# Strassen's products over 1024 tokens instead of 512 for the last four token chunks, with half of g kept in DRAM meanwhile

## The chip, the cores and the metric

The kernel runs on one core of a Trainium2 chip. The metric is the device time of one execution in microseconds (us), lower is better; it is measured several times, and the median is compared. One further execution is recorded by the hardware profiler; its instructions, waits and transfers are what the views of the profile show. Engines are called as there: PE is the matrix engine (PEld its weight loads), DVE the vector engine, ACT the scalar engine, POOL the general one, SP the queue from which nearly all DMAs are issued.

## The reference

Windowed attention over 8 batches and 8 heads of 576 tokens, then a gated feed-forward layer over all 4608 tokens. The part that matters here is the second:

```
x   = attention(q, k, v) as [4608 tokens, 512]
h   = x @ w_in                      # [4608, 2048]
g   = h * erf(softplus(h))
out = g @ w_out                     # [4608, 512]
```

## The kernel before

**Precision.** Every matmul of the feed-forward layer is made of three: each operand is split into a rounded part (hi) and the rest (lo), and hi*hi, hi*lo and lo*hi are summed in PSUM. DVE and ACT make these parts: a copy that rounds gives hi, a subtraction on DVE gives lo.

**Chunks and steps.** The 4608 tokens are taken in nine chunks of 512 (TOK), numbered 0 to 8. A chunk has eight steps (SPC), one for each pair of 128-wide feature tiles of the 2048 features; STEPS lists all 72 in order. In step t PE multiplies the pair's h (mm1, or mm1_fast from chunk 3 on, FAST), DVE takes h out of PSUM (take, take_fast), ACT makes softplus (argument, L664) and erf (table, L667), each with a table load, DVE multiplies both into g (gate, L674) and splits g in ghi (L677) and glo (L678), and PE multiplies g by w_out into four PSUM banks, acc[0] to acc[3], one for each 128 tokens (mm2, L692). mm2 runs two steps behind mm1. A step is two visits of the main loop, x = 2t and 2t+1; each has a part of mm1, then 12 of the step's 24 matmuls of mm2, each 512 columns wide.

**Strassen's products.** From chunk 3 on, the pair of feature tiles is computed by Winograd's form of Strassen's scheme: w_in's pair is cut in two by features and by contraction, x in two by contraction and by tokens (halves of 256 tokens, HN). Seven products replace eight. A product is 6 matmuls (two halves of its contraction by three for hi and lo), 256 columns wide (L639), so 42 such matmuls a step, 24 in the first visit and 18 in the second. Their PSUM banks are h and bank ("tx" in the profile). The sums of w_in are built once, kept in DRAM (ws) and loaded for each step (load_left, 1024 KB and 768 KB). The sums of x are made for each chunk by DVE (right_less, right_lo) and ACT (right_hi) from x loaded by right_load in up to 12 DMAs.

**Attention** is spread over the feed-forward layer. It has 72 units. The table PACE lists the visits x at which two units have their turn ("a visit with attention"): PE turns two units' probabilities (L253), multiplies values (L272) and makes two later units' scores (L214); DVE takes maxima (L225), ACT the exponents (L235), DVE and POOL normalize (L246 to L248). In before the last visit with attention is x = 103, in step 51.

**Order.** All engines run their own instructions in the order in which the code issues them (manual_schedule); SP too starts its DMAs one after the other, and a DMA whose source or room is not ready holds up those behind it. When a chunk's sums are complete, store (L719) copies acc[0] and acc[2] out on DVE, acc[1] and acc[3] on ACT, and sends them to DRAM; between one chunk's last mm2 and the next chunk's first there is always a part of mm1.

Of the kernel before, what the change touches and what calls it, by code (L numbers as in the profile page):

```python
# [18 lines left out]
P = 128  # L19
# [24 lines left out]
SCALE = 0.125  # L44
BIG = 3.0e38

# [10 lines left out]

RUNS = [(0, 0, HALF), (1, 0, SPC), (0, HALF, SPC)] + [(c, 0, SPC) for c in range(2, NCH)]
STEPS = [(c, p, i) for i, (c, a, b) in enumerate(RUNS) for p in range(a, b)]
# [23 lines left out]

PACE = [19, 23, 27, 31, 33, 35, 37, 39, 43, 47, 51, 55, 59, 61, 65, 67, 71, 75, 79, 83, 87, 91, 93, 97, 99, 103]


def visits():


    at = {n - FIRST: [n] for n in range(FIRST, 2 * NBLK + LAG)}  # L90
    n, x = 2 * NBLK + LAG, 2 * HALF + 1
    for k in range(3):
        at[x + 5 * k // 2] = [n + k]
    for x, n in zip(PACE, range(n + 3, NU + LAG, 2)):
        at[x] = [i for i in (n, n + 1) if i < NU + LAG]
    assert max(n for ns in at.values() for n in ns) == NU + LAG - 1
    return at


def ends(t):  # L100

    return t + 1 == NT or STEPS[t][2] != STEPS[t + 1][2]
# [34 lines left out]
def attn_moe_kernel(ctx: ExitStack, tc: tile.TileContext, qk, v, masks, eye, w_in, w_out, out):  # L137
# [29 lines left out]
    pz = [one.tile([P, n], F32, name=f"pT{i}") for i, n in enumerate((2 * P, TOK))]  # L167
    plain = one.tile([P, 2 * TOK], F32, name="plain")

# [48 lines left out]
    def mask_max(u):  # L218

        pr = probs[u] = work.tile([P, 2 * PARTS, KEYS], F32, name="prob", bufs=LAG + 1)  # L220
        nmax = maxes[u] = small.tile([P, 2 * PARTS], F32, name="nmax", bufs=LAG + 1)
        for h in range(2):
            for p in range(PARTS):
                g = PARTS * h + p
                nc.vector.tensor_tensor_reduce(  # L225
                    out=pr[:, g, :], in0=sps[h][:, u % 2, p, :], in1=mask[QUADS.index(kinds(u, p))],
                    scale=-SCALE, scalar=BIG,
                    op0=ALU.add, op1=ALU.min, accum_out=nmax[:, g:g + 1],
                )
# [341 lines left out]
    def load_left(t, j):  # L571
        if t < NT and STEPS[t][0] >= FAST:
            at = slice(0, PART * KIND) if j == 0 else slice(PART * KIND, len(LEFT) * KIND)
            nc.sync.dma_start(out=left(t).bitcast(F32)[:, at], in_=ws[STEPS[t][1]][:, at])

# [50 lines left out]
    def right(x):  # L626

        c, at = divmod(x + READY, 2 * SPC)
        if FAST <= c < NCH:
            for job, *args in JOBS.get(at, ()):  # L630
                job(c, *args)
# [34 lines left out]
    def table(t):  # L666
        nc.scalar.activation(out=ls[t], in_=ls[t], func=AF.Erf)  # L667

    def gate(t, j):

        hc, e = hs[t], ls[t]
        if j == 0:
            gs[t] = []
            nc.vector.tensor_tensor(out=e, in0=hc, in1=e, op=ALU.mult)  # L674
        ghi, glo = (work.tile([P, TOK], F32R, name=n) for n in ("ghi", "glo"))
        gs[t].append((ghi, glo))
        nc.vector.tensor_copy(out=ghi, in_=e[:, j])  # L677
        nc.vector.tensor_tensor(out=glo, in0=e[:, j], in1=ghi.bitcast(F32), op=ALU.subtract)  # L678

    def mm2(t, j):  # L680
        ghi, glo = gs[t][j]
        _, ftp, run = STEPS[t]
        ft = ftp * PAIR + j
        first, last = ftp == RUNS[run][1] and j == 0, ends(t) and j == PAIR - 1
        parts = ((ghi, wout_hi), (ghi, wout_lo)), ((glo, wout_hi),)

        if last:
            parts = (sum(parts, ()),)
        for part in parts:
            for tt in range(TOK // P):  # L690
                for g, w in part:
                    nc.tensor.matmul(acc[tt], g[:, tt * P:(tt + 1) * P], w[:, ft, :],  # L692
                                     start=(first and w is wout_hi and g is ghi),
                                     stop=(last and g is glo))
        if j == PAIR - 1:
            del gs[t]

# [21 lines left out]
    def store(c):  # L719
        last = c == NCH - 1  # L720
        for tt in range(TOK // P):
# [3 lines left out]
            else:  # L725
                if tt == 0:
                    o = doubles(2).bitcast(F32).rearrange("p n w -> p (n w)")[:, 0:DM]
                else:
                    o = io.tile([P, DM], F32, name="w", bufs=4)
                copy_for(tt)(out=o, in_=acc[tt])  # L730
            r = c * TOK + tt * P
            (nc.scalar if last and tt % 2 else nc.sync).dma_start(out=out[r:r + P, :], in_=o)

    with tc.manual_schedule():
# [14 lines left out]

        plan = visits()  # L750

# [9 lines left out]
        todo, scaled, fresh = [], [FIRST - 1], []  # L761
        for x in range(2 * (NT + 2)):
            t, j = divmod(x, 2)
# [60 lines left out]
            load_left(t + 2, j)  # L824
            right(x)
            build(x)
            for n in ns:
# [5 lines left out]
            if x == 4 * SPC - 2:  # L833
                load_x(2, range(twice))
            for u in [u for u in scaled if due[u] == x + 1]:
                scaled.remove(u)
                normalize(u)
            for m in ready:
                finish(m)
        assert not todo and not prep and not staged and not begun and not made and not rest  # L840

# [83 lines left out]
```

## Time and profile before

| | us |
|---|---|
| median of 3 runs | 907.95 (907.29 to 909.37) |
| the profiled execution, its own time | 909.89 |
| the profiled execution, its span | 907.8 |

The span runs from the first to the last instruction; 2.1 us of the profiled execution's own time lie outside it. The own time is 1.94 us above the median of the runs. Rows of a view name line, engine, operation, what is written and read, and the count. In a timeline the first number is the start, the second how long it took; matmuls overlap, so that the distance of two starts, not the length of one, tells what a matmul costs PE's time. In rows of stretches, the numbers are busy times of PE, PEld, DVE, ACT and POOL, then the granted clock of PE, the busy share of the DMA engines and GB/s.

### The profile page before, as it was taken

The page shows a single profiled execution, that of the slowest core. Times are in us where ns is not written, and L with a number is a line of the kernel's source. Part 1 is how long each engine was busy: PE and PEld are TensorE (multiplying, and loading weights), DVE is VectorE, ACT ScalarE, POOL GpSimd, SP SyncE. Part 2 cuts the span into 40 slices and gives each one's busy share as a digit, 9 for nine tenths or more (in the row PEclk, how much of TensorE's full clock was granted, in tenths as well). Part 3 has the DMA queues.
Part 4 walks back from the last instruction along what each step waited for, and adds up shares of the span by engine and source line. Part 5 has one row for each costly group of instructions (what it writes and reads, how often), then busy time and mean ns, then how long its engine had stood idle before and what let it go on. Part 6 is the DMA issues. An engine that isn't in the chain of part 4 may idle for free.

```text
span 907.8 us, 22886 instructions
## 1 busy us (share of the span) xinstructions
PE 886.3 (98%) x9142; PEld 754.2 (83%) x9142; DVE 669.4 (74%) x1703; ACT 600.5 (66%) x1266; POOL 76.9 (8%) x97
## 2 busy tenths in 40 slices
PE   7799999999999999999999999999999999999998
PEld 3467777888887888889988988888988999999996
DVE  5888878876788888667876777678666866776555
ACT  6889879876678687666776676669654644545442
POOL 2312100000011100000100000001000000000000
PEclk9899999999999999999999999999999999999999
DMA  8874444432459688777658765877566546656521
GB/s 276 278 258 151 123 164 130 155 109 94 156 190 330 216 304 296 245 274 233 217 212 284 264 211 189 290 262 256 179 242 230 181 149 230 235 176 205 200 82 47
DMA packets 69450, 188.89 MB, mean 208 GB/s; under 512 B 9184, under 2 KB 17632, under 8 KB 63200
## 3 DMA queue, kind: packets, MB, share of 16 engines
q1 hardware_dynamic: 69056, 186.91, 60.5%
q8 instruction: 72, 1.18, 0.5%
q10 hardware_dynamic: 288, 0.52, 0.1%
q14 instruction: 34, 0.28, 0.1%
HBM read 153.85 MB, written 33.55 MB: 206 GB/s over the span
## 4 chain that ended last, share of the span: by engine, by line
PE 85%; DVE 7%; ACT 3%; DMA 3%; issue 1%; POOL 0%; SPq 0%; DVEq 0%; POOLq 0%; ACTq 0%
PE acc L692 40%; PE h L639 15%; PE tx L639 12%; PE h L518 10%; PE sp L272 3%; PE sp L214 3%; DMA dbl<-in_w_in_dram 2%; PE sp L253 1%; ACT prob L235 1%; PE h L354 1%; DVE s L674 1%; DVE hc L660 1%; PE acc L272 1%; DVE ghi L677 0%; DVE w L455 0%
## 5 line engine op out<-in xcount | busy, mean ns | idle before, releaser
L692 PE MATMUL acc<-wout_hi,ghi 128*128 128x512 f32 x576 | 228.4, 397 | 0.4 <-DVE ghi L677 0.2
L692 PE MATMUL acc<-wout_lo,ghi 128*128 128x512 f32 x576 | 225.6, 392 | 0.0
L664 ACT ACTIVATE s<-hc 128x1024 f32<-128x1024 f32 x72 | 76.5, 1062 | 188.5 <-DVE hc L653 171.1
L692 PE MATMUL acc<-wout_hi,glo 128*128 128x512 f32 x576 | 159.0, 389 | 0.0
L692 PEld LDWEIGHTS acc<-wout_hi,glo 128*128 128x128 f32 x576 | 108.1, 188 | 22.8
L692 PEld LDWEIGHTS acc<-wout_hi,ghi 128*128 128x128 f32 x576 | 108.5, 188 | 20.6 <-DVE ghi L677 0.8
L692 PEld LDWEIGHTS acc<-wout_lo,ghi 128*128 128x128 f32 x576 | 108.6, 189 | 19.6
L248 POOL TENSOR_TENSOR prob<-prob,rinv 128x256 f32<-128x256 f32 x72 | 69.2, 971 | 536.0 <-DVE ssum L246 313.7
L678 DVE TENSOR_TENSOR glo<-s,ghi 128x512 fp32r<-128x512 f32 x144 | 100.0, 694 | 5.5 <-PE acc L692 0.5
L235 ACT ACTIVATE prob<-prob,nmax 128x64 f32<-128x64 f32 x288 | 96.4, 339 | 8.3 <-DVE nmax L225 7.8
L674 DVE TENSOR_TENSOR s<-hc,s 128x1024 f32<-128x1024 f32 x72 | 92.9, 1290 | 9.1 <-ACT s L667 9.0
L639 PE MATMUL h<-win 128*128 128x256 f32 x720 | 98.1, 283 | 0.0
L518 PE MATMUL h<-x,win 128*128 128x512 f32 x384 | 96.6, 393 | 1.5 <-DVE hc L660 1.5
L664 ACT ACT_TABLE_LOAD x72 | 92.4, 1283 | 1.3
L667 ACT ACT_TABLE_LOAD x72 | 92.4, 1283 | 1.3
L639 PEld LDWEIGHTS h<-win 128*128 128x128 f32 x720 | 91.6, 192 | 0.0
L518 PEld LDWEIGHTS h<-x,win 128*128 128x128 f32 x384 | 71.2, 188 | 17.5 <-DVE hc L660 2.3
L667 ACT ACTIVATE s<-s 128x1024 f32<-128x1024 f32 x72 | 76.3, 1060 | 0.8
L677 DVE CAST ghi<-s 128x512 fp32r<-128x512 f32 x144 | 68.4, 475 | 3.1 <-PE acc L692 0.6
L225 DVE CUSTOM_DVE_ANT_0 prob<-sp,cst 128x64 f32<-128x64 f32 x288 | 45.3, 219 | 33.9 <-ACT rows L314 20.8
L314 ACT COPY rows<-sp 128x128 f32<-128x128 f32 (+7 forms) x167 | 27.9, 307 | 57.1 <-PE sp L214 54.9
L649 DVE TENSOR_TENSOR hc<-h,hc 128x512 f32<-128x512 f32 x48 | 33.2, 692 | 41.2 <-PE h L639 40.9
(108 smaller groups left out, 1259.4 us busy)
## 6 DMA issues: line engine op xcount, KB each, us to landing
win<-ws SPq DMA_DIRECT2D x48, 1024.0 KB, 5.8
win<-ws SPq DMA_DIRECT2D x48, 768.0 KB, 4.4
v<-in_v_dram SPq DMA_DIRECT2D x72, 256.0 KB, 4.3
qk<-in_qk_dram SPq DMA_DIRECT2D x48, 272.0 KB, 4.1
dbl<-in_w_in_dram SPq DMA_DIRECT2D x16, 512.0 KB, 4.8
dbl<-in_w_out_dram SPq DMA_DIRECT2D x16, 512.0 KB, 3.7
ws<-x SPq DMA_DIRECT2D x32, 256.0 KB, 4.2
qk<-in_qk_dram SPq DMA_DIRECT2D x24, 288.0 KB, 4.4
```

What stands on the lines that cost most here:

```text
L225: nc.vector.tensor_tensor_reduce(out=pr[:, g, :], in0=sps[h][:, u % 2, p, :], in1=mask[QUADS.index(kinds(u, p))], scale=-SCALE, scalar=BIG ...
L235: nc.scalar.activation(out=probs[u][:, j, :], in_=probs[u][:, j, :], func=AF.Exp, scale=-1.0, bias=nmax[:, j:j + 1], accum_out=sums[u][:, ...
L248: nc.gpsimd.tensor_tensor(probs[u], probs[u], rinv.broadcast_to([P, 2 * PARTS, KEYS]), op=ALU.mult)
L272: nc.tensor.matmul(xp[h * D:(h + 1) * D, qs], vt[ks, s, h, :], pt[ks, h * P + s * STRIP:h * P + (s + 1) * STRIP], start=True, stop=True, t ...
L518: nc.tensor.matmul(h, win_at[:, ftp, j, cc // 2, w, cc % 2, :], x[cc], start=(k == 0 and i == 0), stop=(k == CC - 1 and i == 2))
L639: nc.tensor.matmul((h, bank)[b][:, half * HN:(half + 1) * HN], w[:, k, wi, c, :], x[:, xi, c, :], start=(c == 0 and n == 0), stop=(c == 1 ...
L664: nc.scalar.activation(out=ls[t], in_=hs[t], func=AF.Softplus)
L667: nc.scalar.activation(out=ls[t], in_=ls[t], func=AF.Erf)
L674: nc.vector.tensor_tensor(out=e, in0=hc, in1=e, op=ALU.mult)
L677: nc.vector.tensor_copy(out=ghi, in_=e[:, j])
L678: nc.vector.tensor_tensor(out=glo, in0=e[:, j], in1=ghi.bitcast(F32), op=ALU.subtract)
L692: nc.tensor.matmul(acc[tt], g[:, tt * P:(tt + 1) * P], w[:, ft, :], start=(first and w is wout_hi and g is ghi), stop=(last and g is glo))
```

## The change

Chunks 0 to 4 stay as they are (PAIRED = 5). Chunks 5 to 8 become two pairs, 5 with 6 and 7 with 8. For a pair, the seven products are made over 1024 tokens, so that a token half is a whole chunk of 512: 7 products of 6 matmuls, 512 columns wide, give h of one pair of feature tiles for both chunks, called A (the first chunk) and B (the second). The eight feature pairs of a pair of chunks are eight such batches, d = 0 to 7 and 8 to 15.

There is room in PSUM for one chunk's sums only. So g of A is multiplied by w_out at once, and g of B is written to DRAM (kept_g, 512 KB for each feature pair) and read back later (load_g).

The main loop now ends at step 40's start, and a new loop of 34 periods follows. ITEMS lists what mm2 does in each: the last two steps of chunk 4 (periods 0 and 1), A of the first pair (2 to 9), B of it (10 to 17), A of the second (18 to 25), B of it (26 to 33). Products are made in periods 0 to 7 and 16 to 23 (BIG); periods 8 to 15 and 24 to 33 hold mm2 alone, 24 matmuls. In a period with products, groups of them (third) alternate with quarters of mm2 (6 matmuls). The sums of x for the second pair are made in periods 8 to 15 (AFT), those of the first pair in visits 68 to 79 and period 0 (FORE). load_g of an item is issued two periods ahead, at the period's end; the store of B's g is issued after multiply_big of B.

All attention that went with steps 40 to 51 is moved: PACE has visits at shorter distances up to x = 65, and what remains goes into periods 0 to 4.

The diff, cut to what matters:

```diff
-PACE = [19, 23, 27, 31, 33, 35, 37, 39, 43, 47, 51, 55, 59, 61, 65, 67, 71, 75, 79, 83, 87, 91, 93, 97, 99, 103]
+PACE = [17, 21, 23, 27, 29, 31, 33, 35, 37, 39, 43, 47, 49, 51, 53, 55, 57, 59, 61, 63, 65]
+BIG = {**{d: d for d in range(SPC)}, **{d + SPC: d for d in range(SPC, 2 * SPC)}}
+ORDER = ("A11", "A12", "S2", "S3", "A22", "S1", "S4")
...
+    def big_load(i):
...
+        for place, name in RAW.items():
+            place, k, c = name, int(name[1]) - 1, PAIRED + 2 * i + int(name[2]) - 1
+            for c2 in range(2):
+                a, end = c * TOK, (c + 1) * TOK
+                while a < end:
+                    b, s0 = divmod(a, S)
+                    m = min(end - a, S - s0)
+                    nc.sync.dma_start(out=raw[place][c2][:, a - c * TOK:a - c * TOK + m],
+                                      in_=xT[b][2 * k + c2][:, s0:s0 + m])
+                    a += m
...
+    AFT = {0: [LO["T4"], LO["T1"]], 8: [(big_load, 1)], 9: [LESS["T1"] + (room_v,)],
...
+    ITEMS = [NT - 2, NT - 1] + [(kind_, i * SPC + k) for i in range(2) for kind_ in "AB" for k in range(SPC)]
+
+    def mm1_big(d, k):
+        bank_ = (h, bank)[(7 * d + k) % 2]
...
+        for c in range(2):
+            for n, (wi, xi) in enumerate(((0, 0), (0, 1), (1, 0))):
+                nc.tensor.matmul(bank_, w[:, wi, c, :], x[c][:, xi, :],
+                                 start=(c == 0 and n == 0), stop=(c == 1 and n == 2))
...
+    def multiply_big(kind_, d):
+        e = hs[kind_, d]
+        nc.vector.tensor_tensor(out=e, in0=e, in1=ls[kind_, d], op=ALU.mult)
+        gs[kind_, d] = []
+        if kind_ == "B":
+            nc.sync.dma_start(out=kept_g[d // SPC][d % SPC], in_=e)
+
+    def load_g(item):
+        kind_, d = item
+        if kind_ == "B":
+            e = work.tile([P, PAIR, TOK], F32, name="hc") if d % 4 > 1 else slab(d % 4)
+            nc.sync.dma_start(out=e, in_=kept_g[d // SPC][d % SPC])
+            hs[item] = e
+
+    def split_item(item, j):
+        e = ls[item] if item == NT - 2 else hs[item]
+        split(item, e[:, j], nc.scalar.copy if isinstance(item, tuple) and item[0] == "B" else None)
...
+        if d is None:
+            groups = [()] * 4
+        elif BIG.get(i + 1) is None:
+            groups = [(0, 1, 2), (3, 4), (5, 6), ()]
+        else:
+            groups = [(0, 1), (2, 3), (4, 5), (6,)]
...
+        split_item(item, 1)
+        third(0)
+        jobs(AFT.get(i, ()))
+        quarter()
+
+        third(1)
+        for u in pending:
+            exponents(u)
...
+            for kind_ in "AB":
+                e = ls[kind_, behind_]
+                nc.scalar.activation(out=e, in_=e, func=AF.Erf)
+        quarter()
...
+            multiply_big("A", behind_)
...
+        turn(ready)
+        if ahead is not None:
+            split_item(ahead, 0)
+        last_ = 6 in groups[2]
+        if last_:
+            multiply_big("B", behind_)
+        third(2)
+        if i and behind_ is not None and not last_:
+            multiply_big("B", behind_)
+        quarter()
+
+        third(3)
+        quarter()
+        if done(item) is not None:
+            store(done(item))
+        attend(ready, scored)
+        if d is not None:
+            load_left(NT + d + 2, 1)
+        if i + 2 < len(ITEMS) and isinstance(ITEMS[i + 2], tuple):
+            load_g(ITEMS[i + 2])
...
-        for x in range(2 * (NT + 2)):
+        for x in range(2 * NT):
...
+            jobs(FORE.get(x, ()))
...
+        for i in range(len(ITEMS)):
+            period(i, late)
```

At the first join of A and B, this is how it stands on two engines. On PE, in before, from chunk 7's last sums to chunk 8's first (acc_93 to acc_96 are acc[0] to acc[3], tx and h are the banks of the products):

```order
L692 MATMUL acc_96<-wout_hi,ghi 128x512
L692 MATMUL acc_96<-wout_lo,ghi 128x512
L692 MATMUL acc_96<-wout_hi,glo 128x512
L639 MATMUL tx<-win 128x256 x12
L639 MATMUL h<-win 128x256 x12
L692 MATMUL acc_93<-wout_hi,ghi 128x512
```

On PE, in the changed kernel, from period 9 (A, d = 7) to period 10 (B, d = 0):

```order
L712 MATMUL acc_96<-wout_hi,ghi 128x512
L712 MATMUL acc_96<-wout_lo,ghi 128x512
L712 MATMUL acc_96<-wout_hi,glo 128x512
L712 MATMUL acc_93<-wout_hi,ghi 128x512
L712 MATMUL acc_93<-wout_lo,ghi 128x512
```

No product stands between the last sums of A and the first of B any more. On SP, in before, at the same join of chunks 7 and 8 (win<-ws is load_left):

```order
L574 DMA win<-ws 128x1536
L574 DMA win<-ws 128x2048
L732 DMA out_dram<-dbl_10030 128x512
L732 DMA out_dram<-w 128x512 x3
L574 DMA win<-ws 128x1536
```

On SP, in the changed kernel, from period 8 to period 10 (plain<-xT is the last DMA of big_load, g_112<-hc the store of B's g for d = 7, dbl_8496<-g_112 and dbl_8544<-g_112 are load_g of B for d = 0 and 1):

```order
L776 DMA plain<-xT_108 128x512
L872 DMA g_112<-hc 128x1024
L878 DMA dbl_8496<-g_112 128x1024
L750 DMA out_dram<-o 128x512
L750 DMA out_dram<-w 128x512 x3
L878 DMA dbl_8544<-g_112 128x1024
L878 DMA hc<-g_112 128x1024 x2
```

B's first load stands behind the 12 DMAs of big_load and the store of B's last g, and its second load behind the four stores of A's chunk. On DVE, in the changed kernel, in periods 8 and 9 (hc<-hc,s is multiply_big of B for d = 7, then the second split of A's last g, two sums of x in v_85 and v_86, the first split of B's first g, and store's copies):

```order
L869 TENSOR_TENSOR hc<-hc,s 128x1024
L687 CAST ghi<-hc 128x512
L688 TENSOR_TENSOR glo<-hc,ghi 128x512
L783 TENSOR_TENSOR v_85<-win 128x512
L783 TENSOR_TENSOR v_86<-win 128x512
L688 TENSOR_TENSOR glo<-dbl_8496,ghi 128x512
L748 COPY o<-acc_93 128x512
L748 COPY w<-acc_95 128x512
```

The copies of A's sums out of PSUM stand behind the split of B's first g.

More of the change, by code (lines that the diff above doesn't have):

```diff
@@ L691, in mm2, with mm @@
                 for g, w in part:
[L692 to L696, printed above, removed]
+                    yield dict(out=acc[tt], lhsT=g[:, tt * P:(tt + 1) * P], rhs=w[:, ft, :],
+                               start=(first and w is wout_hi and g is ghi), stop=(last and g is glo))
+    def mm2(t, j):
+        _, ftp, run = STEPS[t]
+        for args in products(t, ftp * PAIR + j, j, ftp == RUNS[run][1] and j == 0, ends(t) and j == PAIR - 1):
+            mm(args)
+    def mm(args):
+        nc.tensor.matmul(args["out"], args["lhsT"], args["rhs"], start=args["start"], stop=args["stop"])
     partial = dram.tile([TOK // P, P, DM], F32, name="partial")
```

194 lines of the change are left out of this document (167 added, 27 removed).

## The prediction

> **What bounds the kernel now.** First the page: its busy shares, then the chain that ended last, then single steps.
>
> ```profile
> PE 886.3 (98%) x9142; PEld 754.2 (83%) x9142; DVE 669.4 (74%) x1703; ACT 600.5 (66%) x1266; POOL 76.9 (8%) x97
> PE 85%; DVE 7%; ACT 3%; DMA 3%; issue 1%; POOL 0%; SPq 0%; DVEq 0%; POOLq 0%; ACTq 0%
> ```
>
> PE is busy 98% of the span, and 85% of the chain that ended last is PE's. DVE and ACT have a quarter and a third of the span free. That says what bounds, not how densely PE works. For that I took one step of chunk 7 without attention, as a stretch and on PE's timeline, and for comparison a visit of chunk 1, where products are 512 columns wide.
>
> ```profile
> 756.25:766.77 10.52, 10.52 (x68) 9.54 (x67) 6.20 (x11) 4.69 (x5) 0.00 (x0) 1.00 0.65 228
> 756.25 1.60 PE L639 MATMUL tx<-win 128*128 128x256 f32 x12
> 757.68 1.60 PE L639 MATMUL h<-win 128*128 128x256 f32 x12
> 759.12 0.40 PE L692 MATMUL acc<-wout_hi,ghi 128*128 128x512 f32 x1
> ...
> 146.77:152.21 5.44, 5.44 (x25) 4.50 (x24) 5.30 (x10) 5.39 (x14) 0.00 (x0) 1.00 0.65 209
> 148.13 1.52 PE L518 MATMUL h<-x,win 128*128 128x512 f32 x6
> 149.49 0.39 PE L692 MATMUL acc<-wout_hi,ghi 128*128 128x512 f32 x1
> ```
>
> The step takes 10.52 us, with no gap on PE, at a granted clock of 1.00, while DVE works 6.20 and ACT 4.69 of it. So a step's time is the sum of its matmuls, and only two things move the end: the time PE needs for its matmuls, and gaps in its row. From start to start, twelve 256-column matmuls take 759.12 − 757.68 = 1.44 us, 0.120 each. Six of 512 columns take 149.49 − 148.13 = 1.36 us, and the visit's 24 take 5.44: 0.2267 each. Twice 0.120 is 0.240: 13 ns more than one of 512.
>
> **Part 1, wider products: −10.2 us.** The last four chunks are 32 steps of 10.52 us, 336.6 us. Afterwards PE has 16 sets of 7 x 6 = 42 matmuls for products and 32 items of 24 for mm2, all 512 wide: (672 + 768) x 0.2267 = 326.4 us. Difference 10.2 us. From the 256-wide matmuls alone it is 672 x 0.0133 = 8.9; the rest goes with the changes between widths, which also end. So 8.9 to 10.2; I take 10.2, since whole stretches show it.
>
> The Trainium skill ("TensorE: Matmul & The Clock Gate", section on 56 against 53.3 ns) gives warm matmuls N columns at 2.4 GHz plus about 2.5 ns fixed each, by which the joining would save 672 x 2.5 ns, 1.7 us. The rows above show 13 ns, so the trace does not agree, and the measured spacing goes into the sum.
>
> **Part 2, the joins of A and B: +9.5 us.** In before, one part of mm1 covers the copying of a chunk's sums:
>
> ```profile
> 660.49 1.69 PE L639 MATMUL tx<-x,win 128*128 128x256 f32 x12
> 660.57 0.68 DVE L730 COPY dbl<-acc 128x512 f32<-128x512 f32 x1
> 661.17 0.68 DVE L730 COPY w<-acc 128x512 f32<-128x512 f32 x1
> 663.45 0.40 PE L692 MATMUL acc<-wout_hi,ghi 128*128 128x512 f32 x1
> ```
>
> PE comes back to acc 2.96 us after the chunk's end. At the start of periods 10 and 26 that cover is gone, and B's first g must come from DRAM. Its load stands on SP behind the store of B's last g, which waits for a long row of work on DVE and ACT. The prices:
>
> ```profile
> L678 DVE TENSOR_TENSOR glo<-s,ghi 128x512 fp32r<-128x512 f32 x144 | 100.0, 694 | 5.5 <-PE acc L692 0.5
> L674 DVE TENSOR_TENSOR s<-hc,s 128x1024 f32<-128x1024 f32 x72 | 92.9, 1290 | 9.1 <-ACT s L667 9.0
> L677 DVE CAST ghi<-s 128x512 fp32r<-128x512 f32 x144 | 68.4, 475 | 3.1 <-PE acc L692 0.6
> L649 DVE TENSOR_TENSOR hc<-h,hc 128x512 f32<-128x512 f32 x48 | 33.2, 692 | 41.2 <-PE h L639 40.9
> L664 ACT ACTIVATE s<-hc 128x1024 f32<-128x1024 f32 x72 | 76.5, 1062 | 188.5 <-DVE hc L653 171.1
> L667 ACT ACT_TABLE_LOAD x72 | 92.4, 1283 | 1.3
> L667 ACT ACTIVATE s<-s 128x1024 f32<-128x1024 f32 x72 | 76.3, 1060 | 0.8
> L609 ACT CAST win<-w 128x512 fp32r<-128x512 f32 x15 | 8.4, 615 | 0.0
> ...
> 902.07 0.69 DVE L730 COPY dbl<-acc 128x512 f32<-128x512 f32 x1 [2.71 <-PE acc L692]
> 902.79 0.34 SPq L732 DMA_DIRECT2D out_dram<-dbl  x1
> ```
>
> I count from the start of period 7 (23 for the second pair). A product or a quarter of mm2 is 6 x 0.2267 = 1.36 us. The period holds 66 matmuls, 14.96 us, and periods 8 and 9 have 24, 5.44 each: period 10 is due at 25.84. PE ends the fifth product at 6 x 1.36 = 8.16. Then DVE has, in its order: the fifth take 0.69, A's multiply 1.29, a split 0.475 + 0.694, B's multiply 1.29, the sixth take (1024 columns; no row has it, the nearest is the multiply's 1.29), the seventh 0.69: 14.6. ACT: softplus of B 1.06, table 1.28, erf of A 1.06: 18.0. DVE: multiply of A 1.29, split 1.17, multiply of B 1.29: 21.7. The last two rows show a handover: the copy ends at 902.76, SP issues at 902.79 and takes 0.34. With that issue, of the store, before the load's, the load starts at 22.1.
>
> ```profile
> dbl<-in_w_in_dram SPq DMA_DIRECT2D x16, 512.0 KB, 4.8
> dbl<-in_w_out_dram SPq DMA_DIRECT2D x16, 512.0 KB, 3.7
> DMA to landing us min/median/max: 3.4/4.8/6.7
> 686.04 7.64 SPq L597 DMA_DIRECT2D win<-xT  x12
> L732 SPq DMA_DIRECT2D out_dram<-w x26: 333/410/1702, 219.4 to 904.2; - x26
> ```
>
> Loads of 512 KB, the size of load_g, land after 3.4 to 6.7 us. With the 512 KB store just ahead I take the larger median, 4.8, for the second pair. In the first pair the 2 MB of big_load are ahead too, issued from about 13 on (they stand behind the store of B's g for d = 6, whose multiply ends at 8.16 + 0.69 + 1.29 + 1.17 + 1.29 = 12.6); I take the middle of 4.8 and 6.7. So the loads land at 26.9 and 27.9. After that ACT makes ghi (0.62), DVE glo (0.69), and only then, by DVE's order, the copy of acc[0] (0.68), with handovers 2.2 us. PE starts at 29.1 and 30.1 instead of 25.84: gaps of 3.3 and 4.2 us.
>
> The second load waits on SP for four stores, the last of which needs copies that end 2.8 us after the first landing; at 0.41 us an issue it starts 3.7 after that landing, lands 4.25 later (middle of the medians), and its ghi is there 0.7 later: at 8.65, when PE, started at 2.2, has ended period 10 at 7.64. Gap 1.0 at each pair. Later loads find four buffers and run ahead. Sum 3.3 + 4.2 + 2 x 1.0 = 9.5. Bounds: all loads at 3.4 give 2 x (1.9 + 0.2) = 4.2; all at 6.7 give 2 x (5.2 + 3.5) = 17.4.
>
> The Trainium skill ("DMA: Bandwidth & Descriptors", anatomy of one DMA) fits 2.0 us plus bytes at 436 GB/s on another queue than SP, an estimated 3.2 us for 512 KB, by which the joins would cost some 3.4 us. No load of that size here landed under 3.4.
>
> **Part 3, hurried attention: +1.2 us.** Each visit's PE work stays the same, but it has to fit in fewer steps: visits only two apart (one step) are seven instead of four before x = 48, and nine instead of two up to x = 65.
>
> ```profile
> 249.62:257.46 7.84, 7.84 (x158) 6.43 (x156) 5.88 (x14) 4.45 (x4) 2.02 (x2) 1.00 0.20 75
> 263.05:271.32 8.27, 8.10 (x158) 6.42 (x156) 7.47 (x17) 5.14 (x8) 2.02 (x2) 1.00 0.66 254
> 276.91:285.66 8.75, 8.10 (x158) 6.42 (x156) 8.14 (x17) 5.87 (x12) 2.02 (x2) 1.00 0.99 356
> 457.43:470.43 13.00, 13.00 (x204) 11.61 (x199) 9.43 (x34) 10.82 (x29) 2.03 (x2) 1.00 0.54 188
> ```
>
> These are x = 33, 35 and 37, in before: the same work takes 7.84, 8.27 and 8.75, so a hurried visit costs 0 to 0.91 while the sums of w_in are built on DVE. The last row is a whole step of chunk 4 with a visit right after another: 10.52 + 2.48, no gap. I take 0.4 for each of the three added early ones and nothing for the seven later ones; bounds 0 and 10 x 0.91 = 9.1.
>
> **Costed at nothing.** Product periods: takes 5 x 0.69 + 0.69 + 1.29, multiplies 2.58, splits 2.34, so DVE has 10.4 of 14.96; ACT 4 x 1.06 + 2 x 1.28 = 6.8. A late visit adds DVE 9.43 − 6.20 = 3.2 and ACT 10.82 − 4.69 = 6.1, and PE 2.48 as before: still under 17.4. A bank is needed again 2.72 us after its product's end, and a take is 0.69. In periods 8 to 15 DVE has two glo and about four sums of x, 4.2 of 5.44. FORE adds 18 x 0.69 = 12.4 us to DVE in steps 35 to 39, which have 5 x 4.3 free. Its 2 MB load of x is issued in x = 68 and first used at the end of x = 70, over a step of 10.52 us later; if it came late, DVE's queue would stand and the next take with it, an estimated 1 to 2 us. Loads of ws halve.
>
> **The sum.** −10.2 + 9.5 + 1.2 = +0.5. On the profiled execution's 909.89 (span 907.8 and 2.1 outside) that is 910.4; this execution lies 1.94 above the median of the runs, 907.95, so I forecast 908.5: no change. A measurement of this kernel tells changes over 0.2%, 1.8 us, from none.
>
> **Rivals.**
> - *The joins are short* (faster): loads at their fastest and no hurried gap give −10.2 + 4.2 = −6.0, 902.0; with part 3 as above 903.1. For it: 3.4 is reached. Against: a store or stores are just ahead of all four loads. It counts as faster once joins and visits cost less than 8.4 together.
> - *big_load holds up B's first load* (slower): 12 DMAs of 1 MB took SP 7.64 us; twice the bytes at that rate take 15.3 from 13.0, so the load starts at 28.3 instead of 22.1, 6.2 later, and the first pair's gap is 10.4: 914.7. It decides from a delay of 1.3 us on. In the meantime DVE would also wait, with the first sum of x, ahead of B's split. Against: eight of the 12 DMAs here are 448 or 512 columns wide, wider than most of those in the row.
> - *Hurried visits* (slower): 0.43 to 0.91 for all ten: 4.3 to 9.1 in place of 1.2, 911.6 to 916.4. It decides from 0.25 a visit. Against: the gapless step of chunk 4.
> - *Wider products save next to nothing* (slower): were the 13 ns not a matmul's fixed price but something that wide products with a new weight each also pay, parts 2 and 3 alone would stand: 907.95 + 10.7 = 918.7. Against: chunk 1's visit, with new weights for each matmul, runs at 0.2267. The Trainium skill's page named above, with its 2.5 ns, sides with this rival; by it the sum would be 917.0.
>
> **How the numbers follow.** Forecast 0.34; short joins 0.31; big_load 0.18; hurried visits 0.15; no saving 0.02. So faster 0.31, same 0.34, slower 0.35. The range leaves out the last microsecond of the short joins, the upper end of the hurried visits and no saving: 903.0 to 916.0.
>
> **What would show it.** Right: L832 matmuls of 512 at 0.2267 from start to start; product periods of 14.96 and 17.4; two gaps of 3 to 4.5 us on PE at the start of periods 10 and 26, ended by DVE's copy of acc, each preceded by the load of g landing 26 to 28 us after the start of period 7 or 23; gaps of about 1 us a period later. Wrong: no such gaps, gaps inside product periods, spacing near 0.24, or many gaps with POOL's prob as releaser between x = 17 and 65.

## The result

The changed kernel takes 917.64 us (median of 4 runs, 916.58 to 918.91), the kernel before 908.66 on the same chip (907.29 to 909.97). The ratio is 1.0100, with a 95% interval from 1.0078 to 1.0121: slower by 9 us. The forecast was 908.5, no change, with a range up to 916.0. The profiled execution's span is 915.8, against 907.8 before: 8.0 more.

### The profile page after: what moved, and what is told of

It is laid out like the page before. It is cut to its first block, busy times and chain, and to the rows that moved or that the text cites. A ratio compares the mean times of both kernels' runs of the same rounds, so it can differ in the third digit from the quotient of the medians.

```text
span 915.8 us, 21525 instructions
## 1 busy us (share of the span) xinstructions
PE 883.7 (96%) x8470; PEld 722.5 (79%) x8470; DVE 644.0 (70%) x1623; ACT 575.5 (63%) x1265; POOL 73.7 (8%) x97
## 4 chain that ended last, share of the span: by engine, by line
PE 74%; DVE 10%; ACT 7%; DMA 6%; issue 2%; SPq 1%; POOL 1%; DVEq 0%; POOLq 0%; ACTq 0%
PE acc L712 33%; PE h L526 10%; PE tx L832 8%; PE h L832 8%; PE h L648 4%; PE sp L280 3%; PE tx L648 3%; PE sp L222 3%; ACT prob L243 2%; PE sp L261 1%; DMA qk<-in_qk_dram 1%; DMA dbl<-in_w_in_dram 1%; DMA dbl<-g 1%; DVE s L681 1%; DMA win<-xT 1%
## 5 line engine op out<-in xcount | busy, mean ns | idle before, releaser
L256 POOL TENSOR_TENSOR prob<-prob,rinv 128x256 f32<-128x256 f32 x72 | 67.3, 940 | 492.8 <-DVE rinv L255 230.6
L673 ACT ACTIVATE s<-hc 128x1024 f32<-128x1024 f32 x40 | 42.5, 1062 | 40.6 <-DVE hc L662 25.1
L322 ACT COPY rows<-sp 128x128 f32<-128x128 f32 (+7 forms) x167 | 27.9, 306 | 51.9 <-PE sp L222 51.2
L688 DVE TENSOR_TENSOR glo<-s,ghi 128x512 fp32r<-128x512 f32 x78 | 54.3, 696 | 2.7
L669 DVE COPY hc<-h 128x512 f32<-128x512 f32 x48 | 33.1, 689 | 30.9 <-PE h L526 30.6
L243 ACT ACTIVATION_READ_ACCUMULATOR prob<-prob,nmax 128x1 f32 x288 | 54.5, 189 | 0.0
L681 DVE TENSOR_TENSOR s<-hc,s 128x1024 f32<-128x1024 f32 x39 | 48.6, 1246 | 5.8 <-ACT s L676 5.8
L832 PE MATMUL tx<-win 128*128 128x512 f32 x192 | 49.1, 391 | 0.0
L832 PE MATMUL h<-win 128*128 128x512 f32 x192 | 49.0, 391 | 0.0
```

What stands on the lines that cost most here:

```text
L243: nc.scalar.activation(out=probs[u][:, j, :], in_=probs[u][:, j, :], func=AF.Exp, scale=-1.0, bias=nmax[:, j:j + 1], accum_out=sums[u][:, ...
L256: nc.gpsimd.tensor_tensor(probs[u], probs[u], rinv.broadcast_to([P, 2 * PARTS, KEYS]), op=ALU.mult)
L669: nc.vector.tensor_copy(out=hs[t][:, j], in_=h)
L673: nc.scalar.activation(out=ls[t], in_=hs[t], func=AF.Softplus)
L681: nc.vector.tensor_tensor(out=e, in0=hs[t], in1=ls[t], op=ALU.mult)
L688: nc.vector.tensor_tensor(out=glo, in0=e, in1=ghi.bitcast(F32), op=ALU.subtract)
```

## The profile after

First the page of the changed kernel: PE's busy share, the granted clock in 40 slices, and the chain that ended last.

```profile
PE 883.7 (96%) x8470; PEld 722.5 (79%) x8470; DVE 644.0 (70%) x1623; ACT 575.5 (63%) x1265; POOL 73.7 (8%) x97
PEclk9899999999999999999999999999998999999999
PE 74%; DVE 10%; ACT 7%; DMA 6%; issue 2%; SPq 1%; POOL 1%; DVEq 0%; POOLq 0%; ACTq 0%
```

PE's share of the chain falls from 85% to 74%; DVE, ACT and the DMAs have gained what it lost. PE has less to do, and waits more. The clock row has one 8 behind the start, in the slice from 687 to 710 us, where the first join lies. So I went there by stretches. Each is one period, from its first matmul of mm2 to the next period's: a product period of the second pair (16), one with late attention (1), the first join (9, 10 and 11) and the second (25 and 26). The columns are the length, the busy times of PE, PEld, DVE, ACT and POOL, then the granted clock, the DMA share and GB/s.

```profile
735.17:750.13 14.96, 14.96 (x67) 12.39 (x66) 6.67 (x9) 6.09 (x7) 0.00 (x0) 1.00 0.36 123
567.32:586.47 19.15, 17.74 (x199) 14.40 (x198) 13.11 (x38) 12.48 (x31) 1.19 (x2) 1.00 0.49 172
687.71:696.95 9.24, 5.60 (x26) 4.35 (x24) 5.10 (x9) 2.09 (x5) 0.00 (x0) 0.95 0.63 216
696.95:705.25 8.30, 8.30 (x24) 6.58 (x25) 4.08 (x7) 3.27 (x8) 0.00 (x0) 0.65 0.93 340
705.25:710.69 5.44, 5.44 (x25) 4.50 (x24) 3.87 (x7) 3.34 (x7) 0.00 (x0) 1.00 0.44 162
857.57:865.75 8.18, 5.60 (x26) 4.35 (x24) 3.89 (x7) 2.09 (x4) 0.00 (x0) 1.00 0.36 128
865.75:872.88 7.13, 7.13 (x25) 5.72 (x25) 1.64 (x3) 1.17 (x3) 0.00 (x0) 0.76 0.88 303
```

The product period takes the forecast 14.96 us, with PE busy all the time. The three other places do not go as they should:

- Period 1 takes 19.15; its matmuls need 14.96 + 2.48 = 17.44. PE is busy 17.74 of it by the row, and stands still otherwise. Periods 2 and 3 take 19.19 and 18.39.
- Periods 9 and 25 should take 5.44. They take 9.24 and 8.18: gaps of 3.80 and 2.74 ahead of B's first matmul.
- Periods 10 and 26 take 8.30 and 7.13 instead of 5.44, although PE is busy from end to end. There the clock is 0.65 and 0.76 in the mean: matmuls run at half speed (0.43 us from start to start instead of 0.227) for a while after each gap.

This is the first join on the engines' timelines in the changed kernel (start, length, engine, line; in brackets how long the engine had been idle, and what ended that).

```profile
689.53 0.44 SPq L878 DMA_DIRECT2D dbl<-g  x1
...
694.86 0.62 ACT L687 CAST ghi<-dbl 128x512 fp32r<-128x512 f32 x1 [8.49 <-DMA dbl<-g]
695.51 0.69 DVE L688 TENSOR_TENSOR glo<-dbl,ghi 128x512 fp32r<-128x512 f32 x1 [4.04 <-ACT ghi L687]
696.12 0.68 DVE L748 COPY o<-acc 128x512 f32<-128x512 f32 x1
...
696.95 0.77 PE L712 MATMUL acc<-wout_hi,ghi 128*128 128x512 f32 x1 [3.64 <-DVE o L748]
...
698.69 0.55 SPq L878 DMA_DIRECT2D dbl<-g  x1
704.07 1.14 ACT L687 CAST ghi<-dbl 128x512 fp32r<-128x512 f32 x2 [5.03 <-DMA dbl<-g]
...
871.64 1.15 ACT L687 CAST ghi<-dbl 128x512 fp32r<-128x512 f32 x2 [5.87 <-DMA dbl<-g]
```

Period 7, counted from its first product as in the prediction, started at 667.31, so B's first load was issued 22.22 after it (forecast 22.1), and its ghi began 27.55 after it (forecast: landing at 27.9). Then come ghi, glo and the copy of acc[0], one behind the other, and PE 2.09 after the landing that ACT's row shows (forecast 2.2). The chain is the one that was written down. The second load was issued only at 698.69, behind the four stores, and its ghi began at 704.07; PE, slowed by the clock, came to need it at 705.25. The last row is the same ghi at the second join, 871.64; PE came to it at 872.88.

The late attention, in period 2, which started at 586.47:

```profile
590.07 2.01 ACT L941 ACTIVATE s<-s 128x1024 f32<-128x1024 f32 x2
591.36 1.22 DVE L869 TENSOR_TENSOR hc<-hc,s 128x1024 f32<-128x1024 f32 x1
592.49 0.17 DVE L254 TENSOR_SCALAR ssum<-ssum 128x4 f32<-128x4 f32 x1
593.04 1.19 POOL L256 TENSOR_TENSOR prob<-prob,rinv 128x256 f32<-128x256 f32 x2 [17.97 <-DVE ssum L254]
593.71 0.20 PEld L261 LDWEIGHTS sp<-ident,prob 128*128 128x128 f32 x2 [1.64 <-POOL prob L256]
```

ACT's row from 590.07 on holds both erf. DVE multiplies A's g (591.36) as soon as the first of them is done, then normalizes (592.49), POOL finishes the probabilities from 593.04 on, and PE's weight load for them has waited 1.64. Such a wait stands in periods 1, 2 and 3.

And the first sum of x, in step 35:

```profile
487.75 10.81 SPq L776 DMA_DIRECT2D win<-xT  x12
498.61 0.91 SPq L776 DMA_DIRECT2D dbl<-xT  x2
499.56 0.90 SPq L776 DMA_DIRECT2D plain<-xT  x2
...
502.55 0.69 DVE L783 TENSOR_TENSOR w<-dbl,win 128x512 f32<-128x512 f32 x1 [4.32 <-DMA dbl<-xT]
...
504.56 0.62 PE L648 MATMUL tx<-x,win 128*128 128x256 f32 x3 [0.93 <-DVE hc L661]
```

big_load's 16 transfers are issued from 487.75 to 500.46, which takes SP 12.7 us. DVE is ready for its first sum at 498.23, 10.5 us after the first issue, and stands 4.32 us until the last of them have landed. The take behind it is late, and PE waits 0.93 for a bank.

## The experiments

Each kernel was timed against the kernel before on the same chip; the changed kernel's own ratio is 1.0100. "Periods 9 to 11" and "25 to 27" are their lengths added, 16.32 each without a wait.

| | median, us | ratio to before, 95% | periods 9 to 11 | 25 to 27 | period 1 |
|---|---|---|---|---|---|
| changed kernel | 917.64 | 1.0100 (1.0078 to 1.0121) | 22.98 | 20.75 | 19.15 |
| early_load | 909.78 | 1.0016 (1.0001 to 1.0032) | 18.74 | 16.32 | 19.17 |
| norm_early | 912.77 | 1.0053 (1.0037 to 1.0069) | 22.30 | 20.57 | 17.51 |
| x_early | 915.90 | 1.0089 (1.0075 to 1.0102) | 22.35 | 20.81 | 19.17 |
| keep_clock | 918.41 | 1.0118 (1.0099 to 1.0137) | 24.77 | 21.06 | 19.15 |
| copies_first | 913.42 | 1.0051 (1.0032 to 1.0071) | 20.55 | 17.85 | 19.17 |
| copies_keep | 910.61 | 1.0021 (1.0010 to 1.0033) | 19.19 | 18.11 | 19.13 |
| three | 901.41 | 0.9927 (0.9909 to 0.9945) | 17.83 | 16.32 | 17.51 |
| four | 898.72 | 0.9898 (0.9880 to 0.9915) | 16.32 | 16.32 | 17.51 |
| hurried_before | 909.73 | 1.0020 (1.0006 to 1.0034) | | | |
| hurried_later | 909.13 | 1.0009 (0.9996 to 1.0022) | | | |

**early_load: B's g is asked for at the start of a period.**

```diff
         split_item(item, 1)
+        if i + 2 < len(ITEMS) and isinstance(ITEMS[i + 2], tuple):
+            load_g(ITEMS[i + 2])
         third(0)
...
             load_left(NT + d + 2, 1)
-        if i + 2 < len(ITEMS) and isinstance(ITEMS[i + 2], tuple):
-            load_g(ITEMS[i + 2])
```

> load_g is issued near the start of a period instead of at its end, so that B's first load stands ahead of big_load and of the store of B's last g, and B's second ahead of the four stores of A's chunk. Theory (the joins cost what they do because B's g comes late, and the half clock behind each gap is a consequence of the gap): the gaps of 3.80 and 2.74 us ahead of periods 10 and 26 shrink to what the copies alone leave, under 1 each, and the granted clock stays at 1.00 in periods 10 and 26, which fall from 8.30 and 7.13 to 5.44; together 9 to 11 us, so 906.5 to 908.5. Rival 1 (the half clock has nothing to do with the gaps): only the gaps go, about 5 to 6.5 us, 911 to 912.5, and periods 10 and 26 stay over 7 us. Rival 2 (the copies out of acc are the limit at the joins, not the load): the gaps stay above 2 us each and the time above 914.

From 1.0100 to 1.0016 is 7.6 us; by the periods of the trace it is 8.7. First the stretches of the four periods at the joins, then DVE's timeline in period 9.

```profile
688.56:696.32 7.76, 5.61 (x26) 4.35 (x24) 5.20 (x9) 3.33 (x7) 0.00 (x0) 1.00 0.94 293
696.32:701.86 5.54, 5.54 (x24) 4.58 (x25) 3.55 (x7) 2.39 (x6) 0.00 (x0) 1.00 0.94 306
854.18:859.62 5.44, 5.44 (x26) 4.50 (x24) 4.25 (x7) 1.21 (x2) 0.00 (x0) 1.00 0.58 203
859.62:865.06 5.44, 5.44 (x26) 4.50 (x24) 1.60 (x3) 2.35 (x4) 0.00 (x0) 1.00 0.98 335
```

```profile
692.82 0.69 DVE L783 TENSOR_TENSOR v<-win 128x512 f32<-128x512 f32 x1 [1.69 <-DMA win<-xT]
694.27 0.69 DVE L783 TENSOR_TENSOR v<-win 128x512 f32<-128x512 f32 x1 [0.77 <-DMA dbl<-xT]
694.88 0.68 DVE L688 TENSOR_TENSOR glo<-dbl,ghi 128x512 fp32r<-128x512 f32 x1
695.48 0.69 DVE L748 COPY o<-acc 128x512 f32<-128x512 f32 x1
```

At the second join nothing is left: 5.44 and 5.44, clock 1.00. At the first a gap of 2.32 stays, and now another wait ends last. B's load had landed before 690.57 (ACT rounds ghi then), but DVE stands in the first sums of x for the second pair until big_load's 2 MB have landed, and the split and the copies stand behind. That was named in the prediction's rival on big_load as a wait "in the meantime"; it came up when the load of g no longer hid it. So the first theory holds for the second join; at the first the expectation (under 1) missed by 1.3. Rival 2, copies as the limit, is refuted at the second join. Rival 1 is settled only by the clock's tally below: the clock stays at 1.00 here, but also behind the 2.32.

**norm_early: the normalization stands ahead of A's multiply.**

```diff
                 mm1_big(d, k)
                 take_big(d, k)
+                while q == 1 and pending:
+                    normalize(pending.pop(0))
...
-        third(1)
         for u in pending:
             exponents(u)
+        third(1)
...
-        while pending:
-            normalize(pending.pop(0))
```

> In the periods with late attention the exponents are issued ahead of the second group of products' takes, and the normalization right after the first take of that group, ahead of A's multiply. Theory (the gap of 1.57 us in each of periods 1 to 3, and most of what periods 0 to 4 take beyond their matmuls, 5.5 us, comes from the normalization that stands on DVE behind A's multiply, which waits for erf, which stands on ACT behind the exponents): the three gaps go and periods 0 to 4 lose 4 to 5.5 us, 912 to 914. Rival (the visits need that time on DVE and ACT wherever the normalization stands, since both add to a period that is already 10.4 of 14.96 busy on DVE): the gap moves to a take or a split, and the time stays within 1.5 us of the changed kernel's 917.6.

From 1.0100 to 1.0053 is 4.3 us. Periods 1 to 3 take 17.51, 17.56 and 16.75 instead of 19.15, 19.19 and 18.39: 4.9 less. Period 1 as a stretch, and POOL's step in period 2, which started at 583.53:

```profile
566.02:583.53 17.51, 17.51 (x200) 14.42 (x199) 13.29 (x38) 12.48 (x31) 1.19 (x2) 1.00 0.54 185
```

```profile
587.60 1.19 POOL L256 TENSOR_TENSOR prob<-prob,rinv 128x256 f32<-128x256 f32 x2 [16.32 <-DVE ssum L254]
588.41 1.45 DVE L869 TENSOR_TENSOR hc<-hc,s 128x1024 f32<-128x1024 f32 x1
```

POOL starts 4.07 after the period's start (587.60 − 583.53) instead of 6.57 (593.04 − 586.47), ahead of A's multiply, and PE does not wait. In period 1 DVE has as much to do as before, 13.29 against 13.11, and ACT the same 12.48. So it was the order on DVE; the rival, that the visits need that time wherever the step stands, falls.

**x_early: big_load two visits earlier.**

```diff
-    FORE = {68: [(big_load, 0)], 70: [LESS["T3"] + (room_w,), HI["B11"]],
+    FORE = {66: [(big_load, 0)], 70: [LESS["T3"] + (room_w,), HI["B11"]],
```

> The first pair's big_load is issued in visit 66 instead of 68. Theory (the gap of 1.09 us on PE ahead of the products at 503, and 0.3 behind it, come from FORE's first sum, which waits 4.32 us on DVE for the last of the 2 MB of x): the gap goes, 1.2 to 1.5 us less, 916.1 to 916.5. Rival (the gap is the work of the jobs on DVE, not the wait): no change, 917.6 within 0.5.

DVE's timeline at the first sum:

```profile
497.99 0.69 DVE L688 TENSOR_TENSOR glo<-s,ghi 128x512 fp32r<-128x512 f32 x1
498.60 0.68 DVE L783 TENSOR_TENSOR w<-dbl,win 128x512 f32<-128x512 f32 x1
```

The wait of 4.32 is gone, the sum follows the split before it at once, and PE has no gap there. The time went from 1.0100 to 1.0089, 1.0 us; the two intervals overlap, so that the runs alone do not tell it. The trace does: from mm2's start in step 33 to its start in step 35 PE takes 22.52 us in the changed kernel and 21.04 here, 1.5 less. The jobs are the same, so the wait is what cost PE its gap.

**keep_clock: PE works while it waits.** The matmuls that are added write a bank that nobody reads.

```diff
         third(3)
         quarter()
+        for _ in range({9: 14, 25: 10}.get(i, 0)):
+            nc.tensor.matmul(h, wout_hi[:, 0, 0:P], wout_hi[:, 0, :], start=True, stop=True)
```

> 14 and 10 matmuls into a bank that nobody reads are added at the end of periods 9 and 25, so that PE works while it waits at the two joins; their result is not used. Theory (the half clock of 6.83 and 3.41 us behind the gaps comes from PE's standing still, and what would stand behind it is B's second load): the granted clock stays at 1.00, periods 10 and 26 fall from 8.30 and 7.13 to 5.44, and gaps of about 2.3 and 1.2 us come up instead at the start of periods 11 and 27, which wait for the second load's ghi; net 0.8 to 1.5 us less, 916.1 to 916.8. Rival 1 (nothing stands behind it): 4.5 us less, 913.1. Rival 2 (the clock falls whatever PE does, for instance by the DMAs or the table loads there): periods 10 and 26 stay at 8.30 and 7.13, time the same, 917.6.

Periods 9, 10, 11, and 25 and 26:

```profile
686.50:696.22 9.72, 8.77 (x40) 6.98 (x38) 5.10 (x9) 2.09 (x5) 0.00 (x0) 1.00 0.63 218
696.22:704.07 7.85, 5.70 (x24) 4.40 (x24) 3.56 (x7) 2.76 (x7) 0.00 (x0) 1.00 0.82 294
704.07:711.26 7.19, 7.19 (x24) 5.75 (x25) 4.38 (x7) 3.88 (x8) 0.00 (x0) 0.76 0.52 194
858.14:866.60 8.46, 7.87 (x35) 6.22 (x34) 3.90 (x7) 2.09 (x4) 0.00 (x0) 1.00 0.37 124
866.60:873.61 7.01, 5.72 (x24) 4.40 (x24) 1.07 (x3) 0.69 (x3) 0.00 (x0) 1.00 0.87 295
```

The clock is 1.00 in periods 10 and 26 now, so it was PE's standing still that halved it: rival 2 falls. This is firm at the first join; at the second alone it would be weak, since gaps of that size were followed by the half clock only every second time (last section). Yet period 10 takes 7.85 with PE busy 5.70 of it, and period 26 7.01: the wait for B's second load, which the slowed matmuls had covered, has come out, 2.4 and 1.6 us over 5.44. Rival 1 falls with that. Nothing was gained: after the wait for the second load the clock halved again, in period 11 (7.19 at 0.76), and B's first loads landed 5.71 and 4.44 us after their issue instead of 5.23 and 4.17, for which these runs show no cause. The ratio of 1.0118 says the same, at or above the changed kernel's; the expected gain of 0.8 to 1.5 did not come.

**copies_first: the copies ahead of B's split.**

```diff
+        late_split = ahead is not None and d is None and done(item) is not None
-        if ahead is not None:
+        if ahead is not None and not late_split:
             split_item(ahead, 0)
...
             store(done(item))
+        if late_split:
+            split_item(ahead, 0)
```

> At the two joins store's copies out of acc are issued ahead of the split of B's first g, so that on DVE and ACT they no longer stand behind the landing of its load. Theory (DVE's order is a part of each gap, and of the second one behind it, since SP issues B's second load behind the stores of those copies): the gaps fall from 3.80 and 2.74 by 1.4 each, to the landing and ghi alone, and B's second load is issued some 3 us earlier, so that periods 10 and 26 fall to 5.4 to 5.9; together 5.5 to 7 us less, 910.5 to 912. Rival 1 (the copies matter, the second loads don't): 2.8 less, 914.8. Rival 2 (the load alone sets the joins): no change.

From 1.0100 to 1.0051 is 4.5 us, by the periods 5.3. Periods 9, 10, 25 and 26:

```profile
687.39:695.34 7.95, 5.61 (x26) 4.32 (x24) 4.97 (x9) 1.85 (x4) 0.00 (x0) 1.00 0.99 354
695.34:702.50 7.16, 7.16 (x25) 5.75 (x25) 4.37 (x7) 3.87 (x8) 0.00 (x0) 0.76 0.93 328
854.82:861.61 6.79, 5.60 (x25) 4.32 (x24) 3.86 (x7) 1.74 (x4) 0.00 (x0) 1.00 0.64 235
861.61:867.19 5.58, 5.58 (x25) 4.55 (x26) 1.42 (x3) 1.26 (x3) 0.00 (x0) 1.00 1.00 325
```

The gaps fall to 2.51 and 1.35, by 1.3 and 1.4 as expected, and behind the second gap period 26 falls from 7.13 to 5.58: B's second load, freed with the stores, is no longer late. Both rivals fall by the trace; the runs alone would leave room for rival 1's 914.8. Period 10 is the miss: 7.16 at a clock of 0.76, where 5.4 to 5.9 was expected.

**copies_keep: the same, with PE kept at work in period 9.**

```diff
         third(3)
         quarter()
+        for _ in range({9: 9}.get(i, 0)):
+            nc.tensor.matmul(h, wout_hi[:, 0, 0:P], wout_hi[:, 0, :], start=True, stop=True)
```

> As copies_first, with 9 matmuls into a bank that nobody reads at the end of period 9; their result is not used. In copies_first period 10 took 7.16 us at a clock of 0.76, though no wait stands in it: B's second g was ready in time. Theory (the half clock comes from PE's standing still for 2.5 us ahead of it, and here, unlike in the changed kernel, nothing hides its price): period 10 falls to 5.4 to 5.6 at a clock of 1.00, 1.6 to 1.7 less than copies_first. Rival (something else in period 10 sets its 7.16): period 10 and the time stay.

```profile
687.01:694.50 7.49, 7.49 (x35) 6.12 (x34) 5.08 (x9) 1.96 (x4) 0.00 (x0) 1.00 0.99 351
694.50:700.63 6.13, 5.63 (x25) 4.32 (x24) 3.59 (x7) 3.11 (x7) 0.00 (x0) 1.00 1.00 339
700.63:706.21 5.58, 5.58 (x25) 4.62 (x26) 4.29 (x7) 3.79 (x8) 0.00 (x0) 1.00 0.57 189
```

Period 10 falls from 7.16 to 6.13 at a clock of 1.00, period 11 takes 0.14 more than 5.44: 0.9 us less over both, not 1.6. The 0.5 that stays in period 10 (PE busy 5.63) is a wait for B's second load, which landed 6.17 us after its issue here and 5.31 in copies_first. In copies_first no such wait lay under the slow matmuls: the ghi of that load began at 699.43, and PE's matmul could begin 0.67 after it (the distance in period 11 here, 699.96 to 700.63), at 700.10, ahead of the 700.78 at which a period of 5.44 would have ended. So the theory holds for copies_first, and copies_keep lost a part of the gain to a later landing. The whole time went from 1.0051 to 1.0021, 2.7 us; the trace's periods give 1.1, and the intervals allow both.

**three and four: everything together.** three has the edits of early_load, norm_early and x_early. four moves the sums of x off the first join as well:

```diff
-    AFT = {..., 8: [(big_load, 1)], 9: [LESS["T1"] + (room_v,)],
-           10: [LESS["T2"] + (room_q,), LESS["T3"] + (room_w,), HI["B11"], HI["B21"]],
-           11: [LESS["T4"] + (room_w,), LO["B11"], HI["T2"], HI["T3"]],
+    AFT = {..., 8: [(big_load, 1)],
+           10: [LESS["T1"] + (room_v,), LESS["T2"] + (room_q,), HI["B11"], HI["B21"]],
+           11: [LESS["T3"] + (room_w,), LESS["T4"] + (room_w,), LO["B11"], HI["T2"], HI["T3"]],
```

> The earlier loads of g, the earlier normalization and the earlier load of x together. Theory (they mend different places, so their gains add): 8.7 by the periods 9 to 11 and 25 to 27 of the first, 4.9 by the periods 1 to 3 of the second and 1.4 to 1.7 of the third, 15 to 15.3 less than the changed kernel's 917.6: 902.3 to 902.7, about 5 less than the kernel before. Rival (one gain gives another's place away): 905 or more.

> As three, and the first sums of x for the second pair are made one period later, in 10 instead of 9, the third group in 11 instead of 10. Theory (the gap of 2.31 us that the earlier loads left at the first join is DVE standing in that sum until the last of the 2 MB of x have landed, with the split and the copies behind it): the gap falls below 0.6, 1.7 to 2.3 less than three, 900.2 to 900.8. Rival (the transfers are what is late there, and the second load of g or the sums in 11 take it up): within 0.5 of three.

Three's gap at the first join is 1.39, four's is none. Periods 9, 10, 26 and 1 of four:

```profile
680.94:686.38 5.44, 5.44 (x25) 4.50 (x24) 4.25 (x7) 1.21 (x2) 0.00 (x0) 1.00 0.94 246
686.38:691.82 5.44, 5.44 (x25) 4.50 (x24) 4.00 (x7) 4.52 (x9) 0.00 (x0) 1.00 1.03 406
849.58:855.02 5.44, 5.44 (x25) 4.50 (x24) 1.60 (x3) 2.35 (x4) 0.00 (x0) 1.00 0.97 337
565.47:582.98 17.51, 17.51 (x200) 14.42 (x199) 13.28 (x38) 12.48 (x31) 1.19 (x2) 1.00 0.52 179
```

No stretch of PE is idle there. The gains add: 901.41 was 0.9 below what was expected of three, 898.72 was 1.5 below that of four. Some 0.9 of this may be the kernel's end: in the profiled executions of both the last store landed 2.1 us after its issue, in the changed kernel's 3.0. Four is 1.0% faster than the kernel before (0.9898, 0.9880 to 0.9915), 9.3 us, close to the 10.2 that the wider products were to save: with the waits gone, the change gives what was worked out for it, and this is the best version of the study.

**hurried_before and hurried_later: hurried attention alone, in the kernel before.**

```diff
-PACE = [19, 23, 27, 31, 33, 35, 37, 39, 43, 47, 51, 55, 59, 61, 65, 67, 71, 75, 79, 83, 87, 91, 93, 97, 99, 103]
+PACE = [17, 21, 23, 27, 29, 31, 33, 35, 37, 39, 43, 47, 49, 51, 53, 55, 57, 59, 61, 63, 65, 67, 71, 75, 79, 83]
```

hurried_later ends with 71, 77, 83, 89, 95 instead.

> The kernel before with visits with attention at 17, 21, 23, 27, 29, and so on, as in the changed kernel up to 65, and the last five at 67, 71, 75, 79 and 83: hurried attention alone, nothing else of the change. The forecast: 1.2 us slower. The rival of hurried visits: 4.3 to 9.1 slower. The reading of the changed kernel's trace (one more gap, of 0.29, and the three early ones as long as before): 0 to 0.5 slower, not to be told from none.

> As hurried_before (the kernel before with the changed kernel's visits with attention up to 65), but the last five visits at 71, 77, 83, 89 and 95. It is to tell whether the 1.8 us that the runs of hurried_before showed (interval 0.5 to 3.1) are real, since its trace shows only 0.26 from 51 us on and 1.07 in the first 51 us, where the two kernels issue the same work. If the trace is right: 0 to 0.5 slower than before, the interval holding 1.000. If the hurried visits cost what the runs said: again 1.3 to 2.3 slower.

Visits of hurried_before: one that does not wait (x = 61), then x = 63 and 37.

```profile
439.90:447.18 7.28, 7.28 (x163) 6.38 (x161) 5.20 (x13) 7.22 (x14) 1.23 (x2) 1.00 0.73 260
452.90:460.57 7.67, 7.52 (x163) 6.36 (x162) 6.52 (x14) 4.92 (x6) 2.02 (x2) 1.00 0.70 256
282.51:291.29 8.78, 8.10 (x157) 6.42 (x156) 8.14 (x17) 5.89 (x12) 2.03 (x2) 1.00 1.01 346
```

x = 37 takes what it took before (8.75), and x = 63 takes 0.39 more than a visit that does not wait. From the first matmul of mm1 to the end the span is 0.26 longer than before's, that of hurried_later 0.06. The runs say 1.8 (0.5 to 3.1) and, for hurried_later, 0.8 (−0.4 to 2.0). The rival's 4.3 to 9.1 falls. Between 0.3 and 1.2 the runs do not decide, and I take the trace's 0.3.

## Why the prediction was wrong

By its own steps, on the profiled executions, whose difference is +8.0:

- **Wider products, −10.2: right.** The product periods take 14.96, the mm2 periods 5.44, and four without its waits is 9.3 us faster than before.
- **Joins, +9.5: the mechanism right, the size 1.6 short.** Periods 9 to 11 are 22.98 − 16.32 = 6.7 too long, 25 to 27 20.75 − 16.32 = 4.4: 11.1. The first loads' gaps were 3.80 and 2.74 (forecast 4.2 and 3.3). What was mis-sized is the second loads, put at 1.0 each; what was missing is the half clock that follows a gap. Both lie over each other in periods 10 and 26, which are 2.86 and 1.69 too long, and the rows tell them apart. Wherever PE waited for a second load (norm_early, x_early, keep_clock, at both joins), its matmul began 0.67 to 0.68 us after that load's ghi. In the changed kernel the ghi began at 704.07 and 871.64, so at full clock PE would have gone on at 704.74 and 872.31 instead of 705.25 and 872.88. By this estimate the half clock cost 0.5 and 0.6, and the second loads the rest, 2.35 and 1.1. keep_clock uncovers 2.4 and 1.6, with landings of its own.
- **Late visits, costed at nothing: the step that failed.** The sentence was "A late visit adds DVE 9.43 − 6.20 = 3.2 and ACT 10.82 − 4.69 = 6.1, and PE 2.48 as before: still under 17.4." The sums were right, DVE had 13.1 to do in 19.15. But room in a period says nothing about when a short step gets its turn: normalize stood behind A's multiply, that behind erf, that behind the exponents, and PE needed the outcome before the period's middle. norm_early gives it back: 4.9. Without this step's error the time would have lain inside the stated range (norm_early 912.77).
- **The load of x for the first sum, costed at nothing: failed.** "Over a step of 10.52 us later" was right as a distance (487.75 to 498.23), but it is too short for 2 MB: SP took 12.7 us to issue them, and they landed 4.32 after DVE wanted them. The prediction's own rate, 7.64 us for 1 MB, gives 15.3 for 2 MB; it was used for the other load, in a rival, and not here. "An estimated 1 to 2 us" if late, given without a working, was right: 1.5 by the trace, 1.0 by x_early's runs.
- **Hurried attention, +1.2:** 0.3 by the trace, not settled by the runs. The prediction counts two visits right after another between x = 48 and 65 in the kernel before; its table has one (59 to 61). The later ones were taken at nothing, so 1.2 stays, but the upper bound would be 10.0, not 9.1.
- **Rivals.** big_load did not delay B's load (22.22 against 22.1), so that rival fell as put; its side remark, DVE's wait in the first sum of x, turned up as soon as the load was mended. Short joins fell too. Wider products without a saving (918.7 and 917.0) come nearest to the measured 917.64, but by chance: the product periods take 14.96, and four has the saving.

So +0.5 becomes −10.2 + 11.1 + 4.9 + 1.5 + 0.3 = +7.6. Outside these places the two profiled executions differ by another 0.3: the last stores landed 3.0 us after their issue instead of 2.1, which lengthens the end by 0.95, and the first matmul of mm1 came at 50.13 instead of 50.81. That makes 7.9 of the 8.0. In norm_early, three and four the last store landed after 2.1 again. What sets that was not tried. The sign of the error is no accident: two terms stood at nothing because an average left room for them, and a wait on the bounding engine can only cost.

## What to carry to other kernels

When work is moved into a tighter stage, busy shares tell only whether it fits; walk the in-order queue of each engine to the short step that the bounding engine waits for, and price the step by what stands ahead of it. Ask for data that comes back from DRAM before anything else that is issued in that stage, and keep the copies that free a bank ahead of work that waits for the data. When a stall is mended, look again at the same place: behind the late load of g stood the copies, behind them the sums of x, and over all of them a slower clock that hid a second late load. And price a load by the time its issues take, too: the one that had a whole step's time came late because the issues alone took longer.

## What the runs showed of the hardware

**The clock halves behind short gaps, and not always.** Stand-stills of PE late in the kernel, taken as the period's length less its matmuls, over the changed kernel and the eight variants of it: of 3.6 to 3.8 us (changed kernel, norm_early, x_early) all three were followed by matmuls 0.43 us apart instead of 0.227; of 2.3 to 2.9 us three of six were (2.74 in the changed kernel at the second join, 2.51 in copies_first, 2.41 in keep_clock ahead of period 11) and three were not (2.32 in early_load, 2.66 in norm_early and 2.85 in x_early at the second join); of 1.6 us and less none. The slow stretch lasted 2.6 to 5.9 us. The Trainium skill ("TensorE: Matmul & The Clock Gate", Part 1) has PE fall to half rate after an idle window of some 3.4 us, and says that the window runs free, so that the count of slow matmuls varies between runs. The variation agrees, 2.6 to 5.9 us here; but three gaps of 2.4 to 2.7 us were followed by the half clock, so that a gap below that figure was not safe here.

**What a half clock costs depends on what stands behind it.** In periods 10 and 26 of the changed kernel PE was busy to the full and slow, and most of what it would have saved at full speed it would have spent waiting for the next transfer: of 2.86 and 1.69 us some 0.5 and 0.6 are the clock's own, by the estimate above. In copies_first the next g was ready, and period 10's 1.7 us are the clock's in full. A low granted clock is a symptom to be priced by what stands behind it.
